# First chunk of a fused attention and MoE kernel: the gate's order, a copy of h, and where the weights' operations stand in a step

## The chip, the core and the metric

The kernel runs on one core of a Trainium2 chip. The metric is the device time in microseconds (us), the median of a few executions. TensorE (PE in the rows; PEld is its loading of weights), VectorE (DVE), ScalarE (ACT), GpSimd (POOL) and SyncE (SP, which here only issues DMAs) each work through a queue of their own in order, and wait for one another by semaphores. ScalarE's queue also issues some of the DMAs (ACTq in the rows).

## What is computed

Block-sparse attention over 4 batches of 768 positions and 8 heads of 64, and then an MLP over the 3072 tokens:

```python
def _moe_ref(x, w_in, w_out) -> np.ndarray:
    h = x @ w_in
    g = h * (1.0 / (1.0 + np.exp(-1.702 * h)))
    return (g @ w_out).astype(np.float32)
```

with x the attention's output (3072 x 512), w_in 512 x 2048 and w_out 2048 x 512. The gate h * sigmoid(1.702 h) is computed as h * (1 + tanh(0.851 h)), and the factor 0.5 is put on the output. The weights arrive as 64-bit numbers whose two 32-bit words have to be made into one fp32 number, and each fp32 number is split into a high part that TensorE's fast format holds and the rest, so that a product takes three matmuls.

## The kernel before

The 3072 tokens are six chunks of 512. A chunk's MLP is 16 steps of one 128-wide slice f of the hidden dimension; over all chunks they are steps m = 0 to 95, and `tick(m)` writes one step. Step m computes h for its slice in PSUM bank 7 (`up`, 12 matmuls in two halves, L491 to L493; rows of the built order call that bank bank_92), applies the gate (`gate`: tanh by ScalarE at L499, then (tanh + 1) * h by VectorE at L500, which reads h from the bank), rounds g to its high part by ScalarE (`gate_hi`, L505), and multiplies the slice of the step before into the output's four banks (`down(m - 1, 0)`, 8 matmuls at L535 and L536 with the high part of g; `down(m - 1, 1)`, 4 matmuls at L531 with the rest of g, which VectorE makes at L513 at the start of a step, `gate_lo`). There is one bank for h in all chunks but the last, so `up(m + 1)` can't begin before all readers of step m's h are done.

While a chunk's MLP runs, the attention for the next chunk is laid between its steps by `plan`, in quarters of a step: scores (L260) and values (L331) on TensorE in one step, transposes of the probabilities (L306) and the turn of the result (L384) in the next. Through steps 1 to 11 the scores and values open the odd steps, the transposes and the turn the even ones. With them go VectorE's minima (L283) and ScalarE's exponentials (L290) in odd steps, and ScalarE's copies `pt` of the transposes (L310), two tiny factors, and the pair xhi (ScalarE, L391) and xlo (VectorE, L392) of the finished rows in even ones. From step 12 on the plan is denser and its parts stand in other quarters.

The first chunk has more to do: the weights are made ready in it. `weights` is a generator; each `next` of it issues one operation, and four make a tile: a shift on VectorE (L446, with a 512 KB DMA for a later tile from ScalarE's queue, L414); VectorE's rest of the tile before (L427, with a DMA that saves it in DRAM when it is a wout tile, L433); VectorE's merge (L452, with ScalarE's Abs of the next tile, L422, into one of three buffers `a`); VectorE's second merge (L456, with ScalarE's rounding cast that waits for it, L459). There are 32 tiles, 16 win that stay and 16 wout in a ring of three, and about seven of them are done before step 0. When the ring is full the generator yields without an operation. A step in the first chunk issues up to five of these operations at its end, and in steps without scores four more ahead of the gate (`n0`, `n1`). What is left is issued ahead of step 16. From step 16 on a step reads a saved wout tile back (`stream`, `split`, tiles `wst`, two buffers).

The functions that the diff touches:

Of the kernel before, what the change touches and what calls it, by code (L numbers as in the profile page):

```python
# [9 lines left out]
F32 = mybir.dt.float32  # L10
# [3 lines left out]
ALU = mybir.AluOpType  # L14
# [4 lines left out]
P = 128  # L19
# [5 lines left out]
DM = H * D  # L25
DF = 2048
NCT = DM // P
NF = DF // P
# [9 lines left out]
QT = 4  # L38
# [5 lines left out]
class Kernel:  # L44
# [448 lines left out]
            nc.tensor.matmul(h, wil[:, k], hi[:, k], start=False, stop=(k == NCT - 1))  # L493
        self.h = h

    def gate(self, m):
        nc = self.nc
        g = self.work.tile([P, CT], F32, name="g")
        nc.scalar.activation(out=g, in_=self.h, func=AF.Tanh, scale=0.851)  # L499
        nc.vector.scalar_tensor_tensor(out=g, in0=g, scalar=1.0, in1=self.h, op0=ALU.add, op1=ALU.mult)  # L500
        self.g[m] = [g]

    def gate_hi(self, m):
# [107 lines left out]

    def tick(self, m):

        n0, n1 = 0, 0
        if m < NF:
            heavy = any(part == self.scores for q in range(QT) for part, g in self.at.get(QT * m + q, ()))
            n0, n1 = (0, 5) if heavy else (4, 5)

        def run(n):
            for _ in range(n):  # L620
                next(self.conv, None)

        def finish(todo):
            for f in todo:
                f()

        moe = m < NC * NF
        self.gate_lo(m - 1)
        finish(self.begin(QT * m))
        if moe:  # L630
            self.up(m, range(0, 2))
        finish(self.begin(QT * m + 1))
        if moe:
            self.up(m, range(2, 4))
        run(n0)
        after = self.begin(QT * m + 2)
        if moe:
            self.gate(m)
        finish(after[:2])
        self.down(m - LAG, 0)  # L640
        if moe:
            self.gate_hi(m)
        finish(after[2:])
        finish(self.begin(QT * m + 3))
        self.down(m - LAG, 1)
        self.split(m + 1)
        self.stream(m + 3)
        run(n1)

    def first(self):  # L650

# [93 lines left out]
```

## Time and profile before

| what | value |
|---|---|
| median of 3 executions | 797.04 us (796.22 to 797.87) |
| the profiled execution's own time | 797.87 us |
| its span, first to last instruction | 796.2 us |
| PE busy | 742.6 us, 93% |
| DVE busy | 413.5 us, 52% |
| ACT busy | 377.4 us, 47% |
| mean granted clock of TensorE | 0.981 of full speed |

Busy shares are averages over the whole span. The first chunk's MLP runs from about 75 us (step 0) to 210 us (step 16 begins); there the three engines are loaded otherwise than later, since the weights' operations are all before that. A step's beginning is read off TensorE's first L491 of it: 87.32 for step 2, 101.77 for step 4, 118.43 for 6, 135.60 for 8, 151.67 for 10, 169.71 for 12, 188.72 for 14, 209.96 for 16.

### The profile page before, as it was taken

To read this page: it belongs to the slowest core of one execution; us is meant where nothing else is said; L and a number is where in the kernel's file an instruction comes from. 1 tells how busy PE (TensorE), PEld (TensorE's weight loads), DVE (VectorE), ACT (ScalarE), POOL (GpSimd) and SP (SyncE) were. 2 spreads that over 40 slices of the span, in tenths; PEclk is the share of its full clock that TensorE was granted. 3 is DMA by queue.
4 is the path that set the end of the run, shared out by engine and by line. 5 is a ranking of instruction groups with operands and counts; after the bars stand their busy time and mean duration, and the time that the engine had idled before them with its cause. 6 is when DMAs were issued, how large, how long until landed. Compare 5 with 4: busy or idle time off the path is not lost.

```text
span 796.2 us, 19245 instructions
## 1 busy us (share of the span) xinstructions
PE 742.6 (93%) x7584; PEld 574.4 (72%) x7584; DVE 413.5 (52%) x1076; ACT 377.4 (47%) x937; POOL 56.6 (7%) x85
## 2 busy tenths in 40 slices
PE   2567998998899999999999999999999999999996
PEld 0445876776677777778778787787787777788885
DVE  3387777887554444454444544544464443443332
ACT  0576565565445454454454445444554545333232
POOL 5122100001000000000000000000000000000000
PEclk9798999999999999999999999999999999999999
DMA  8999676767474355674354465453574231131212
GB/s 262 287 351 329 208 251 204 247 201 236 140 228 154 103 174 135 184 197 144 116 181 123 127 184 142 138 155 108 170 249 166 67 90 58 40 96 50 54 40 53
DMA packets 61116, 128.21 MB, mean 161 GB/s; under 512 B 7569, under 2 KB 26514, under 8 KB 60514
## 3 DMA queue, kind: packets, MB, share of 16 engines
q1 hardware_dynamic: 46882, 80.50, 34.3%
q0 software_dynamic: 7232, 25.51, 9.8%
q10 hardware_dynamic: 6912, 20.97, 8.0%
q8 instruction: 60, 0.98, 0.5%
q14 instruction: 30, 0.25, 0.1%
HBM read 116.47 MB, written 10.49 MB: 159 GB/s over the span
## 4 chain that ended last, share of the span: by engine, by line
PE 76%; DVE 9%; ACT 6%; DMA 4%; issue 3%; ACTq 1%; POOL 0%; SPq 0%; POOLq 0%; DVEq 0%
PE bank L491 10%; PE bank L531 10%; PE bank L535 10%; PE bank L536 9%; PE bank L493 9%; PE bank L492 9%; PE bank L306 5%; PE bank L260 4%; PE bank L331 4%; ACT ex L290 2%; DMA ws<-a 2%; PE bank L339 2%; PE bank L272 2%; DVE a L452 2%; DVE a L456 2%
## 5 line engine op out<-in xcount | busy, mean ns | idle before, releaser
L500 DVE SCALAR_TENSOR_TENSOR g<-g,bank 128x512 f32<-128x512 f32 x96 | 66.0, 687 | 199.0 <-ACT g L499 198.9
L491 PE MATMUL bank<-xhi,win 128*128 128x512 f32 x384 | 159.5, 415 | 5.9 <-DVE g L500 5.7
L535 PE MATMUL bank<-wout,ghi 128*128 128x512 f32 x384 | 154.8, 403 | 0.0
L536 PE MATMUL bank<-wout,ghi 128*128 128x512 f32 x384 | 152.6, 397 | 2.2 <-DVE wout L427 2.2
L290 ACT ACTIVATE ex<-bank,nm 128x256 f32<-128x256 f32 (+1 forms) x208 | 99.5, 491 | 113.8 <-DVE nm L283 112.0
L493 PE MATMUL bank<-xhi,win 128*128 128x512 f32 x384 | 151.7, 395 | 0.2 <-DVE win L427 0.2
L492 PE MATMUL bank<-xlo,win 128*128 128x512 f32 x384 | 150.8, 393 | 0.0
L499 ACT ACTIVATE g<-bank 128x512 f32<-128x512 f32 x96 | 57.4, 598 | 145.1 <-PE bank L493 142.0
L531 PE MATMUL bank<-wout,glo 128*128 128x512 f32 x384 | 108.2, 395 | 0.5 <-DVE glo L513 0.5
L480 DVE TENSOR_TENSOR wout<-wst,wout 128x512 fp32r<-128x512 f32 x80 | 55.4, 692 | 84.1 <-ACT wout L479 83.1
L491 PEld LDWEIGHTS bank<-xhi,win 128*128 128x128 f32 x384 | 72.6, 189 | 24.1 <-DVE g L500 7.8
L283 DVE CUSTOM_DVE_ANT_1 bank<-bank,bias 128x256 f32<-128x256 f32 x176 | 73.8, 440 | 25.5 <-PE bank L260 17.3
L505 ACT CAST ghi<-g 128x512 fp32r<-128x512 f32 x96 | 59.7, 621 | 56.2 <-DVE g L500 56.2
L536 PEld LDWEIGHTS bank<-wout,ghi 128*128 128x128 f32 x384 | 72.9, 190 | 18.3 <-DVE wout L427 2.6
L531 PEld LDWEIGHTS bank<-wout,glo 128*128 128x128 f32 x384 | 72.7, 190 | 18.3 <-DVE glo L513 1.0
L493 PEld LDWEIGHTS bank<-xhi,win 128*128 128x128 f32 x384 | 72.6, 189 | 17.2 <-DVE win L427 0.6
L535 PEld LDWEIGHTS bank<-wout,ghi 128*128 128x128 f32 x384 | 72.5, 189 | 16.1
L492 PEld LDWEIGHTS bank<-xlo,win 128*128 128x128 f32 x384 | 72.9, 190 | 13.2
L216 POOL DMA_INDIRECT vown<-in_v_dram,vidx x44 | 43.3, 984 | 508.8 <-PE bank L331 397.4
L260 PE MATMUL bank<-kg,qt 64*32 64x256 f32 x1408 | 54.8, 409 | 20.4 <-DMA kg<-in_kb_dram 13.6
L310 ACT COPY pt<-bank 128x512 f32<-128x512 f32 (+1 forms) x120 | 61.2, 563 | 20.2 <-PE bank L306 19.7
L513 DVE TENSOR_TENSOR glo<-g,ghi 128x512 fp32r<-128x512 f32 x96 | 65.7, 685 | 1.4 <-ACT ghi L505 1.4
(73 smaller groups left out, 782.4 us busy)
## 6 DMA issues: line engine op xcount, KB each, us to landing
wst<-ws SPq DMA_DIRECT2D x80, 256.0 KB
kg<-in_kb_dram SPq DMA_DIRECT2D x136, 128.0 KB
kg<-in_kb_dram SPq DMA_DIRECT2D x22, 384.0 KB
raw<-in_moe_w_in_dram ACTq DMA_DIRECT2D x16, 512.0 KB
raw<-in_moe_w_out_dram ACTq DMA_DIRECT2D x16, 512.0 KB
kg<-in_kT_dram SPq DMA_DIRECT2D x4, 1536.0 KB
vown<-in_vd_dram SPq DMA_DIRECT2D x8, 768.0 KB
qt<-in_q_dram SPq DMA_DIRECT2D x22, 256.0 KB
```

The source lines that it names most:

```text
L260: nc.tensor.matmul(sps[h][BLK * c:BLK * (c + 1), n * i:n * (i + 1)].rearrange("p (n s) -> p n s", s=BLK), self.qt[r][rows, bi, UT * pair + ...
L283: nc.vector.tensor_tensor_reduce(out=at, in0=at, in1=bias, scale=-SCALE, scalar=3.0e38, op0=ALU.add, op1=ALU.min, accum_out=un["nm"][:, ha ...
L290: nc.scalar.activation(out=ex, in_=sps[h][:, n * k:n * (k + 1)], func=AF.Exp, bias=un["nm"][:, half, c:c + 1], scale=-1.0, accum_out=un["r ...
L310: copies.append(lambda pt=pt, ps=ps, m=m: nc.scalar.copy(out=pt[:, 0:m], in_=ps[:, 0:m]))
L491: nc.tensor.matmul(h, wih[:, k], hi[:, k], start=(k == 0), stop=False)
L492: nc.tensor.matmul(h, wih[:, k], lo[:, k], start=False, stop=False)
L493: nc.tensor.matmul(h, wil[:, k], hi[:, k], start=False, stop=(k == NCT - 1))
L500: nc.vector.scalar_tensor_tensor(out=g, in0=g, scalar=1.0, in1=self.h, op0=ALU.add, op1=ALU.mult)
L513: self.nc.vector.tensor_tensor(out=glo, in0=g, in1=ghi.bitcast(F32), op=ALU.subtract)
L531: nc.tensor.matmul(o[n], glo[:, tk[n]], woh, start=False, stop=last)
L535: nc.tensor.matmul(o[n], ghi[:, tk[n]], woh, start=(f == 0), stop=False)
L536: nc.tensor.matmul(o[n], ghi[:, tk[n]], wol, start=False, stop=False)
```

## The change

In the first chunk's steps 0 to 12 ScalarE copies h out of the bank right after tanh, into a buffer of the pool `wst`, and the gate's product reads that copy; in steps 13 to 15 and in all later chunks it reads the bank as before. The weights' operations of a step are put in three places: three right after the first quarter's pt copies and factors (only in steps without scores; the xhi and xlo pair now comes after them), three between tanh and the gate's product, and three at the step's end. That is 6 in a step with scores and 9 in one without; before, it was 5 and 9.

```diff
-    def gate(self, m):
+    def gate(self, m, between):
         nc = self.nc
         g = self.work.tile([P, CT], F32, name="g")
         nc.scalar.activation(out=g, in_=self.h, func=AF.Tanh, scale=0.851)
-        nc.vector.scalar_tensor_tensor(out=g, in0=g, scalar=1.0, in1=self.h, op0=ALU.add, op1=ALU.mult)
+        h = self.h
+        if m < NF - 3:
+
+            h = self.work.tile([P, DM], F32, name="wst")
+            nc.scalar.copy(out=h, in_=self.h)
+        between()
+        nc.vector.scalar_tensor_tensor(out=g, in0=g, scalar=1.0, in1=h, op0=ALU.add, op1=ALU.mult)
         self.g[m] = [g]
...
-        n0, n1 = 0, 0
+        n0, n1, n2 = 0, 0, 0
         if m < NF:
             heavy = any(part == self.scores for q in range(QT) for part, g in self.at.get(QT * m + q, ()))
-            n0, n1 = (0, 5) if heavy else (4, 5)
+            n0, n1, n2 = (0, 3, 3) if heavy else (3, 3, 3)
...
         moe = m < NC * NF
         self.gate_lo(m - 1)
-        finish(self.begin(QT * m))
+        after = self.begin(QT * m)
+        finish(after[:3])
+        run(n0)
+        finish(after[3:])
         if moe:
             self.up(m, range(0, 2))
         finish(self.begin(QT * m + 1))
         if moe:
             self.up(m, range(2, 4))
-        run(n0)
         after = self.begin(QT * m + 2)
         if moe:
-            self.gate(m)
+            self.gate(m, lambda: run(n1))
         finish(after[:2])
         self.down(m - LAG, 0)
         if moe:
...
         self.split(m + 1)
         self.stream(m + 3)
-        run(n1)
+        run(n2)
```

TensorE's and GpSimd's instructions keep their order; VectorE has as many as before in another order, ScalarE 13 more. Two places show the move. In the rows `bank_92` is h's bank, `win_101` to `win_116` are the win tiles 0 to 15, `wout_117` to `wout_119` the ring.

ScalarE in step 10 (an even one, without scores), before, from the pt copies to the high part of g:

```order
L310 COPY pt<-bank_85 128x512
L310 COPY pt<-bank_86 128x512
L391 CAST xhi_122<-bank_87 128x4x64
L414 DMA raw<-in_moe_w_in_dram 128x1024
L433 DMA ws_79<-a 128x512
L422 ACTIVATE a<-raw 128x512
L459 CAST win_113<-a 128x512
L499 ACTIVATE g<-bank_92 128x512
L505 CAST ghi<-g 128x512
```

and the same stretch now:

```order
L310 COPY pt<-bank_85 128x512
L310 COPY pt<-bank_86 128x512
L422 ACTIVATE a<-raw 128x512
L459 CAST win_113<-a 128x512
L414 DMA raw<-in_moe_w_out_dram 128x1024
L391 CAST xhi_122<-bank_87 128x4x64
L499 ACTIVATE g<-bank_92 128x512
L504 COPY wst<-bank_92 128x512
L422 ACTIVATE a<-raw 128x512
L459 CAST wout_119<-a 128x512
L511 CAST ghi<-g 128x512
```

The cast of win tile 12, which stood right ahead of tanh, now stands two places earlier; behind tanh comes the copy of h, and between it and the high part of g an Abs and a cast of the next tiles. On VectorE the same step went from shift, rest, merge, merge ahead of the gate's product to three operations ahead of xlo and three behind it.

VectorE in step 14, before, from its x to the minima of step 15; `wout_119` here is wout tile 14, which `down(14)` in step 15 reads:

```order
L373 TENSOR_TENSOR x<-bank_87,ri 128x256
L500 SCALAR_TENSOR_TENSOR g<-g,bank_92 128x512
L446 TENSOR_SCALAR a<-a 128x512
L427 TENSOR_TENSOR win_116<-a,win_116 128x512
L452 SCALAR_TENSOR_TENSOR a<-raw,a 128x512
L456 SCALAR_TENSOR_TENSOR a<-raw,a 128x512
L446 TENSOR_SCALAR a<-a 128x512
L513 TENSOR_TENSOR glo<-g,ghi 128x512
```

and now:

```order
L373 TENSOR_TENSOR x<-bank_87,ri 128x256
L446 TENSOR_SCALAR a<-a 128x512
L427 TENSOR_TENSOR wout_119<-a,wout_119 128x512
L452 SCALAR_TENSOR_TENSOR a<-raw,a 128x512
L506 SCALAR_TENSOR_TENSOR g<-g,bank_92 128x512
L456 SCALAR_TENSOR_TENSOR a<-raw,a 128x512
L427 TENSOR_TENSOR wout_117<-a,wout_117 128x512
L519 TENSOR_TENSOR glo<-g,ghi 128x512
```

The rest of wout tile 14 now stands in step 14, ahead of the gate's product; before, it stood behind the gate's product of step 15. The last tile's rest (`wout_117`) is issued in step 14 too, and no weights' operation is left behind it.

## Rows read from the trace of the kernel before

**Rows 1.** Busy time by stretch, steps 2 to 16, two steps a row

```profile
core 0: us, PE busy (x) PEld busy (x) DVE busy (x) ACT busy (x) POOL busy (x), PEclk, DMA share, GB/s
87.32:101.77 14.45, 14.45 (x157) 11.42 (x156) 10.70 (x27) 7.85 (x20) 2.67 (x2) 1.00 0.78 241
101.77:118.43 16.66, 15.21 (x157) 11.34 (x155) 13.35 (x31) 9.71 (x23) 0.00 (x0) 1.00 0.75 245
118.43:135.60 17.17, 14.93 (x154) 11.45 (x155) 13.04 (x31) 9.88 (x23) 1.88 (x2) 1.00 0.72 231
135.60:151.67 16.07, 15.26 (x154) 11.36 (x154) 13.41 (x31) 9.86 (x23) 0.00 (x0) 1.00 0.73 227
151.67:169.71 18.04, 16.13 (x155) 12.62 (x155) 13.91 (x32) 10.48 (x24) 1.87 (x2) 0.91 0.68 215
169.71:188.72 19.01, 17.35 (x253) 13.10 (x251) 14.05 (x34) 10.82 (x26) 0.00 (x0) 1.00 0.68 208
188.72:209.96 21.24, 17.48 (x162) 12.67 (x155) 15.54 (x39) 11.11 (x30) 2.48 (x2) 0.92 0.62 198
```

**Rows 2.** Waits from 101.77 to 209.96: total us, times, longest

```profile
DVE g L500 <- ACT g L499: 13.6, 10, 2.3
...
PEld bank L491 <- DVE g L500: 7.4, 8, 2.1
...
DVE xlo L392 <- ACT xhi L391: 3.5, 4, 1.0
...
DVE wout L427 <- ACT wout L459: 2.4, 6, 0.7
...
DVE win L427 <- ACT win L459: 2.1, 6, 0.4
```

**Rows 3.** Timelines by engine, step 10: start, us, what, [idle before, releaser]

```profile
154.31 0.40 PE L493 MATMUL bank<-xhi,win 128*128 128x512 f32 x1
...
159.58 0.62 ACT L459 CAST win<-a 128x512 fp32r<-128x512 f32 x1 [2.19 <-DVE a L456]
160.11 0.59 ACT L499 ACTIVATE g<-bank 128x512 f32<-128x512 f32 x1
...
160.73 0.69 DVE L500 SCALAR_TENSOR_TENSOR g<-g,bank 128x512 f32<-128x512 f32 x1 [1.18 <-ACT g L499]
...
161.47 0.71 PE L491 MATMUL bank<-xhi,win 128*128 128x512 f32 x1 [1.91 <-DVE g L500]
```

**Rows 4.** Timelines of VectorE and TensorE in step 15

```profile
205.00 0.68 DVE L427 TENSOR_TENSOR wout<-a,wout 128x512 fp32r<-128x512 f32 x1
...
205.74 0.62 PE L536 MATMUL bank<-wout,ghi 128*128 128x512 f32 x1 [2.15 <-DVE wout L427]
```

**Rows 5.** Forms of L500, L480 and L310: busy us, mean ns, idle before

```profile
L500 DVE SCALAR_TENSOR_TENSOR g<-g,bank 128x512 f32<-128x512 f32 x96 | 66.0, 687 | 199.0 <-ACT g L499 198.9
...
L480 DVE TENSOR_TENSOR wout<-wst,wout 128x512 fp32r<-128x512 f32 x80 | 55.4, 692 | 84.1 <-ACT wout L479 83.1
...
L310 ACT COPY pt<-bank 128x512 f32<-128x512 f32 x88 | 47.4, 591 | 20.2 <-PE bank L306 19.7 <-ACT wout L459 0.3 <-issue 0.2
```

**Rows 6.** Timelines of ScalarE and TensorE in steps 13 and 15

```profile
184.29 0.66 ACT L422 ACTIVATE a<-raw 128x512 f32<-128x512 f32 x1 [2.47 <-DMA ws<-a]
...
199.16 1.58 PE L260 MATMUL bank<-kg,qt 64*32 64x256 f32 x32 [1.28 <-ACT pt L310]
```

**Rows 7.** Saving DMAs and the Abs behind them: chain, then ScalarE's timeline

```profile
177.93 6.28 DMA ws<-a
...
101.72 0.33 ACTq L433 DMA_DIRECT2D ws<-a  x1
...
105.38 0.69 ACT L422 ACTIVATE a<-raw 128x512 f32<-128x512 f32 x1
...
128.59 0.97 ACTq L433 DMA_DIRECT2D ws<-a  x1
...
136.37 0.67 ACT L422 ACTIVATE a<-raw 128x512 f32<-128x512 f32 x1 [0.17 <-DMA ws<-a]
```

## The prediction

> **What bounds the kernel now.** The page gives TensorE 93% of the span, so I went to the stretches where it isn't gapless: the windows of two steps each through the first chunk. Steps 2 and 3 took 14.45 us with TensorE busy for all of it, and that is the floor for two such steps. The next four pairs hold the same TensorE work and took 16.66, 17.17, 16.07 and 18.04 us, 67.94 in place of 57.80; the two after them, 19.01 and 21.24 [rows 1]. VectorE is the busiest beside TensorE there: 13.04 to 13.91 us a pair.
>
> The waits say what fills the rest. Over 101.77 to 209.96 (six pairs) VectorE waits 13.6 us for tanh ahead of the gate's product, 3.5 for xhi, and 2.4 + 2.1 for the weights' casts: 2.27 + 1.33 us a pair [rows 2]. With its mean busy time in the four pairs, (13.35 + 13.04 + 13.41 + 13.91) / 4 = 13.43, that makes 17.03 a pair, and the four took 16.98 on average. So VectorE is never free there: it works, or stands at the gate's product, or waits for a rounding. TensorE follows it, and waits 7.4 us for h's bank [rows 2].
>
> Step 10 shows how. Its last h matmul starts at 154.31 and lasts 0.40, so h is there at 154.71. But tanh starts only at 160.11: ahead of it in ScalarE's queue stands a weights' cast that itself stood 2.19 us for VectorE's merge. The product at 160.73 lets go of the bank, and the next step's first matmul starts at 161.47 after 1.91 us of nothing [rows 3]. The granted clock then drops; its mean is 0.91 in that pair, which is 0.09 x 18.04 = 1.6 us of TensorE's time [rows 1].
>
> **The change, part by part.**
>
> *The gate's order and the copy.* In odd steps (with scores) VectorE now has three weights' operations between tanh and the product instead of none, in even ones three as well, with the other three ahead of xlo. Three operations are about 2 us of VectorE's work, as one pass over 128 x 512 takes 0.69 [rows 5]; tanh and copy are 0.59 + 0.59 [rows 3, 5]. So the 2.27 us a pair of waiting for tanh is covered. I take all of it away; the lower end is that it only moves to another instruction. The bank is let go by ScalarE's copy, not by the product, so TensorE's wait for it goes in steps 1 to 13, unless tanh is itself late. In odd steps tanh still stands behind four exponentials, and there 0.59 of copy replaces 0.69 of product, hardly a gain by itself; the exponentials only come sooner because VectorE does.
>
> *One more operation a pair.* 6 + 9 = 15 weights' operations a pair instead of 5 + 9 = 14: at most 0.69 us more of VectorE, the same total being done earlier.
>
> *Four pairs.* 16.98 - 2.27 + 0.69 = 15.4 us, against the floor of 14.45; times four is 61.6, so -6.3 us. The ends: 0 if the wait returns elsewhere, -10.1 at the floor. Steps 2 and 3 are on the floor already: 0.
>
> *Thirteen copies.* 128 x 512 from PSUM by ScalarE: 0.59 us [rows 5], 13 x 0.59 = 7.7 us. I cost them at nothing, since ScalarE is busy for 9.71 to 10.48 us of a pair [rows 1] and 1.2 more leaves 3.7 of 15.4. What lies behind a copy in the queue is a cast or an Abs, then the rounded g, which `down` reads only in the next step. If that cover were gone, the price is up to 7.7.
>
> Does the product get cheaper with h in SBUF? It took 687 ns with h in PSUM; a pass of the same shape with both inputs in SBUF took 692 [rows 5]. I take 0. [...]
>
> *Steps 12 to 16.* 19.01 + 21.24 us [rows 1]. In step 15 the rest of wout tile 14 runs at 205.00, behind that step's gate; TensorE waits 2.15 us for it [rows 4], and the clock's mean in that pair is 0.92, another 0.08 x 21.24 = 1.7 [rows 1]. The new order has this operation one step earlier, ahead of step 14's product: -3.8 us, the firmest single term. Two more stalls lie here: 2.47 us of ScalarE at an Abs in step 13, which waits for a saving DMA out of its buffer, with tanh and the pt copies behind it, and 1.28 us of TensorE for pt copies in step 15 [rows 6]. The second stood behind a weights' cast that is now done earlier. I credit 0.9 of these 3.7 us, as the Abs in step 13 now again stands ahead of the pt copies. Together -4.7; the ends are 0 and -7.5. In steps 13 to 15 there is no copy, so three operations delay the bank; they cover the tanh, and step 14's following `down` of 12 matmuls hides the rest: 0.
>
> *Later chunks* keep their order: 0. *DMAs*: the same ones, from the same queues, closer together; the DMA share was 0.78 in the pair that ran at the floor [rows 1], so the pace itself is affordable.
>
> *Sum.* -6.3 - 4.7 = -11.0. From the profiled execution, 797.87, that is 786.9; it lies 0.83 above the median 797.04, from which it is 786.0. I predict **786.0**; with both ends, 779.4 to 797.
>
> **Rivals.**
>
> *The saving DMAs eat half of it (792.5).* Abs of a new tile needs a buffer whose saving DMA has landed. One save took 6.28 us and one 7.8 (issued 128.59, its Abs at 136.37 waited for it until then), yet another Abs ran 3.66 us after its save without waiting [rows 7]. In the new order save and Abs are five operations apart, evenly laid: 5 / 15 x 15.4 = 5.1 us. If all took 6.28, each costs ScalarE 1.2 us, with some 1.9 saves a pair 2.2; with half of it passed on to VectorE a pair takes 16.5. Then the four pairs give -2 and the end some -2.5: 792.5.
>
> *All waits gone (779.4).* Every pair at 14.45 and all three stalls of the end away: -10.1 - 7.5. Against it: VectorE would have 14.12 us of work in 14.45.
>
> *The change doesn't free the bank sooner (797).* If tanh stays as late as before, behind the exponentials and the first three operations' cast, copy and product end alike and VectorE waits elsewhere. For it: in step 10 a cast still stands ahead of tanh in the new order. Against it: three operations instead of four lie ahead, and the product has others to cover it.
>
> *Slower, by the same saves (801).* If a save lands after 8.2 us, an Abs waits 3.1, 5.9 us a pair; half of it on VectorE makes 15.4 + 2.95 = 18.35, 5.5 more over the four pairs, and 1.5 or so comes back at the end. It decides from where half of 1.9 x (landing - 5.1) is more than the 1.6 us gained a pair: 6.8 us for the mean save. One of the three shown is above that.
>
> *Slower, by the copies (804.7).* [...] As a mechanism of this kernel: the copies lie on the path and bring nothing, 13 x 0.59 = 7.7 us. The rows speak against it, because what is waited for is the bank and tanh's place in the queue, not the pass.
>
> **How the numbers follow.** Chances: the forecast (780.5 to 791) 0.60; half eaten 0.20; floor 0.06; no change 0.06; slower by saves 0.05; slower by copies 0.03. The first two make the range, 780.5 to 794, which leaves 0.2 out. 0.2% of the time is 1.6 us, about what a measurement of this kernel can tell from no change. Faster by more than that 0.86, within 0.06, slower 0.08.
>
> **What the changed profile would show.** In the four middle pairs, 15 to 16 us each, found between TensorE's first L491 of steps 4, 6, 8, 10 and 12. In the waits of that stretch, the gate's product for tanh from 13.6 us to under 4, and L491's wait for h's bank under 2. No wait of `down(14)` for wout tile 14, and step 16 beginning near 199. VectorE's busy time the same, ScalarE's 7 to 8 us more. The prediction is wrong if the Abs' waits for saving DMAs grow past about 1 us a save, if the pairs stay above 16.5, or if a new wait of TensorE for the rest of g (L531) appears, since VectorE would then be late by its own work.

## The result, and the profile of the changed kernel

The changed kernel takes 785.01 us (median of 782.75 to 786.06), the kernel before 796.63 us in the same comparison (795.33 to 797.87). The ratio is 0.9851, with a 95% interval of 0.9822 to 0.9879. The forecast was 786.0.

The two profiled executions differ by 15.1 us of span (796.2 to 781.1), more than the medians do (11.6), since that of after is the quickest of its runs and that of before the slowest of its own. The 15.1 lie in four places, read off TensorE's first L491 of a step: 0.77 ahead of step 4, 7.82 in the four pairs of steps 4 to 11, 6.14 in steps 12 to 16, 0.37 behind that.

The windows of the changed kernel, two steps a row, with the columns of [rows 1] and the boundaries at its own steps:

```profile
86.56:101.00 14.44, 14.44 (x157) 11.43 (x156) 12.53 (x30) 10.07 (x24) 1.87 (x2) 1.00 0.87 258
101.00:115.45 14.45, 14.45 (x157) 11.43 (x156) 11.95 (x29) 10.03 (x25) 0.00 (x0) 1.00 0.80 249
115.45:131.08 15.63, 15.23 (x158) 11.35 (x156) 14.08 (x33) 10.69 (x26) 2.39 (x2) 1.00 0.79 260
131.08:145.55 14.47, 14.47 (x155) 11.45 (x155) 13.59 (x33) 10.97 (x25) 0.00 (x0) 1.00 0.77 254
145.55:161.12 15.57, 15.18 (x158) 11.34 (x156) 12.86 (x30) 10.58 (x25) 2.75 (x2) 1.00 0.77 244
161.12:180.65 19.53, 17.95 (x251) 13.25 (x251) 16.53 (x38) 13.65 (x30) 0.00 (x0) 1.00 0.78 256
180.65:195.23 14.58, 14.58 (x161) 11.52 (x155) 10.87 (x32) 8.79 (x26) 2.34 (x2) 1.00 0.67 210
```

Two of the four pairs stand on the floor of 14.45 us, and two are 1.1 to 1.2 above it. The last row is gapless, where before it held the wait for wout tile 14, and the granted clock is 1.00 in all rows. The pair of steps 12 and 13 is now the longest and 0.5 us longer than before.

The waits from 101.00 to 195.23, to be read beside [rows 2]:

```profile
DVE g L506 <- ACT g L499: 1.4, 1, 1.4
DVE g L506 <- ACT wst L504: 0.3, 1, 0.3
...
DVE xlo L392 <- ACT xhi L391: 4.4, 5, 1.2
...
PEld bank L491 <- ACT wst L504: 0.6, 2, 0.3
...
PE bank L260 <- ACT pt L310: 1.5, 2, 1.3
...
ACT a L422 <- DMA ws<-a: 2.6, 4, 1.0
```

The product's wait for tanh went from 13.6 to 1.4 us (0.3 more for the copy), TensorE's wait for h's bank from 7.4 to 0.6. The Abs waited 2.6 us for saving DMAs, in four waits. Of the prediction's other signs, step 16 begins at 195.2 (near 199 was forecast), and ScalarE's busy time over the whole span is 383.5 us against 377.4, so 6.1 more and not 7 to 8.

The timeline of step 10, to be read beside [rows 3]:

```profile
148.16 0.40 PE L493 MATMUL bank<-xhi,win 128*128 128x512 f32 x1
...
151.01 0.62 ACT L459 CAST win<-a 128x512 fp32r<-128x512 f32 x1 [1.42 <-DVE a L456]
...
151.80 0.60 ACT L499 ACTIVATE g<-bank 128x512 f32<-128x512 f32 x1
...
152.29 0.59 ACT L504 COPY wst<-bank 128x512 f32<-128x512 f32 x1
...
153.44 0.50 PE L491 MATMUL bank<-xhi,win 128*128 128x512 f32 x1
...
154.20 0.68 DVE L506 SCALAR_TENSOR_TENSOR g<-g,wst 128x512 f32<-128x512 f32 x1
```

Tanh still stands behind a cast that waited for VectorE, and starts 3.24 us after h is there (5.40 before). But the product doesn't wait, since VectorE had the three operations to do, and the next step's matmul starts ahead of the product, 0.56 us after the copy's end.

Wout tile 14's rest and its reader, in VectorE's and TensorE's timelines (steps 14 and 15), beside [rows 4]:

```profile
184.45 0.69 DVE L427 TENSOR_TENSOR wout<-a,wout 128x512 fp32r<-128x512 f32 x1
...
192.43 0.39 PE L541 MATMUL bank<-wout,ghi 128*128 128x512 f32 x1
```

It is there 7.3 us ahead of its reader, which waits for nothing. The stall that is left is in step 12, in TensorE's timeline:

```profile
165.43 1.58 PE L260 MATMUL bank<-kg,qt 64*32 64x256 f32 x32 [1.30 <-ACT pt L310]
```

The forms of the product and of the copy, beside [rows 5]:

```profile
L506 DVE SCALAR_TENSOR_TENSOR g<-g,bank 128x512 f32<-128x512 f32 x83 | 57.1, 687 | 183.8 <-ACT g L499 183.8
...
L506 DVE SCALAR_TENSOR_TENSOR g<-g,wst 128x512 f32<-128x512 f32 x13 | 8.9, 686 | 4.0 <-ACT wst L504 4.0
L504 ACT COPY wst<-bank 128x512 f32<-128x512 f32 x13 | 7.7, 594 | 0.0
```

### The profile page after: what moved, and what is told of

Its sections match the earlier page's. It is cut to its first block, busy times and chain, and to the rows that moved or that the text cites. A ratio compares the mean times of both kernels' runs of the same rounds, so it can differ in the third digit from the quotient of the medians.

```text
span 781.1 us, 19264 instructions
## 1 busy us (share of the span) xinstructions
PE 738.6 (95%) x7584; PEld 571.7 (73%) x7584; DVE 412.8 (53%) x1076; ACT 383.5 (49%) x950; POOL 57.1 (7%) x85
## 4 chain that ended last, share of the span: by engine, by line
PE 78%; DMA 7%; DVE 7%; ACT 4%; issue 2%; SPq 1%; ACTq 0%; DVEq 0%
PE bank L491 11%; PE bank L541 10%; PE bank L542 10%; PE bank L537 10%; PE bank L493 10%; PE bank L492 10%; PE bank L260 5%; PE bank L306 4%; PE bank L331 4%; DMA ws<-a 3%; DMA kg<-in_kb_dram 2%; PE bank L339 2%; PE bank L272 2%; DMA raw<-in_moe_w_in_dram 2%; DVE a L452 1%
## 5 line engine op out<-in xcount | busy, mean ns | idle before, releaser
L491 PE MATMUL bank<-xhi,win 128*128 128x512 f32 x384 | 158.4, 412 | 1.2 <-ACT xhi L391 0.9
L506 DVE SCALAR_TENSOR_TENSOR g<-g,bank 128x512 f32<-128x512 f32 x83 | 57.1, 687 | 183.8 <-ACT g L499 183.8
L480 DVE TENSOR_TENSOR wout<-wst,wout 128x512 fp32r<-128x512 f32 x80 | 55.4, 693 | 79.7 <-ACT wout L479 78.7
L491 PEld LDWEIGHTS bank<-xhi,win 128*128 128x128 f32 x384 | 72.1, 188 | 18.7 <-ACT xhi L391 1.1
L542 PEld LDWEIGHTS bank<-wout,ghi 128*128 128x128 f32 x384 | 72.5, 189 | 15.6
L310 ACT COPY pt<-bank 128x512 f32<-128x512 f32 (+1 forms) x120 | 61.1, 563 | 19.4 <-PE bank L306 19.3
L331 PEld LDWEIGHTS bank<-vown,pt 128*32 128x32 f32 x1408 | 43.8, 113 | 31.8 <-ACT pt L310 16.0
```

Source lines behind the costliest of these rows:

```text
L310: copies.append(lambda pt=pt, ps=ps, m=m: nc.scalar.copy(out=pt[:, 0:m], in_=ps[:, 0:m]))
L331: nc.tensor.matmul(av[BLK * c:BLK * (c + 1), 0, 2 * i + h], g["pt"][h][:, 2 * i + k, BLK * c:BLK * (c + 1)], src[:, at:at + D], start=(k = ...
L491: nc.tensor.matmul(h, wih[:, k], hi[:, k], start=(k == 0), stop=False)
L542: nc.tensor.matmul(o[n], ghi[:, tk[n]], wol, start=False, stop=False)
```

## The experiments

The theory behind the forecast was: VectorE sets the pace, the operations between tanh and the product fill its wait, the copy frees the bank, and the fifteenth operation a pair brings wout tile 14 in time. The rivals give the whole gain to one of these parts. The table has all kernels. "Steps 4 to 11" and "12 to 15" are windows of TensorE between its first weight load at L491 of steps 4, 12 and 16; "products" is the time from the gate's product of step 3 to that of step 11 on VectorE, four pairs of VectorE's own pace.

| kernel | median us (range) | ratio to before | steps 4 to 11 | 12 to 15 | products |
|---|---|---|---|---|---|
| before | 796.63 (795.33 to 797.87) | 1 | 67.93 | 40.05 | 67.10 |
| changed | 785.01 (782.75 to 786.06) | 0.9851 (0.9822 to 0.9879) | 60.15 | 33.88 | 62.47 |
| the same again | 785.26 (784.14 to 790.22) | 0.9862 (0.9827 to 0.9897) | 59.73 | 33.88 | 62.10 |
| copy alone | 801.79 (801.31 to 803.29) | 1.0084 (1.0066 to 1.0101) | 70.54 | 40.00 | 70.23 |
| order, no copy | 784.95 (783.82 to 785.94) | 0.9864 (0.9842 to 0.9885) | 63.97 | 31.37 | 64.37 |
| copy made, not read | 785.83 (785.21 to 786.83) | 0.9854 (0.9826 to 0.9883) | 63.83 | 32.03 | 64.40 |
| two copies | 791.62 (790.26 to 793.76) | 0.9939 (0.9915 to 0.9964) | 63.82 | 35.41 | 64.31 |
| 14 a pair | 783.88 (783.75 to 785.17) | 0.9860 (0.9838 to 0.9881) | 57.81 | 36.45 | 59.59 |
| 14, no copy | 785.38 (782.45 to 786.58) | 0.9845 (0.9813 to 0.9876) | 57.86 | 35.75 | 58.96 |
| 14, then 16 | 785.25 (783.17 to 787.96) | 0.9854 (0.9829 to 0.9879) | 57.81 | 39.07 | 59.56 |
| 14, then 15 | 783.95 (779.41 to 785.61) | 0.9830 (0.9800 to 0.9861) | 57.82 | 33.82 | 58.79 |
| n0 late | 786.66 (785.36 to 787.13) | 0.9886 (0.9867 to 0.9905) | 63.42 | 33.87 | 65.48 |
| steps without scores | 791.75 (788.58 to 792.60) | 0.9929 (0.9905 to 0.9953) | 62.67 | 37.99 | 63.72 |
| steps with scores | 787.76 (786.73 to 790.10) | 0.9892 (0.9869 to 0.9914) | 62.23 | 34.90 | 62.22 |

The windows are of one profiled execution each, so the medians and the windows need not agree to the tenth. Each ratio is to the kernel before in runs on the same chip. Its median there was 796.63 us for the changed kernel; 796.19 for the copy alone, the order alone, 14 a pair and n0 late; 796.96 for two copies, the two kernels with one kind of step, and "14, then 16"; 797.23 for the other four. Gains below are against these, so small differences between kernels of different rows are better read from the ratios.

**The copy alone.** The kernel before, with this:

```diff
-        nc.vector.scalar_tensor_tensor(out=g, in0=g, scalar=1.0, in1=self.h, op0=ALU.add, op1=ALU.mult)
+        h = self.h
+        if m < NF - 3:
+            h = self.work.tile([P, DM], F32, name="wst")
+            nc.scalar.copy(out=h, in_=self.h)
+        nc.vector.scalar_tensor_tensor(out=g, in0=g, scalar=1.0, in1=h, op0=ALU.add, op1=ALU.mult)
```

> The kernel before with the copy alone: steps 1 to 13 copy h to SBUF by ScalarE behind tanh and the product reads the copy; the weights' operations keep their places. Theory (VectorE paces a pair, and the copy only pays once VectorE's wait for tanh is filled): the pair stays near 17 us, the product still waits some 13 us for tanh in all, now also for the copy; 793 to 798 us. Rival (what TensorE waits for is the bank, and the copy alone gives it back): the 7.4 us of waits of the first h matmul go, 789 to 791 us. Rival (copies cost): 13 x 0.59 = 7.7 us more, 804 us.

It is slower than before, by 5.6 us, so the rival that gives the gain to the copy is refuted, and the theory's range (793 to 798) was too low as well: 801.79 lies nearer to the rival with the full price (804), as the copy costs 5.6 of the 7.7 us. Step 10 in its timelines of ScalarE, VectorE and TensorE shows why:

```profile
164.03 0.62 ACT L459 CAST win<-a 128x512 fp32r<-128x512 f32 x1 [2.13 <-DVE a L452]
164.55 0.59 ACT L499 ACTIVATE g<-bank 128x512 f32<-128x512 f32 x1
165.04 0.58 ACT L504 COPY wst<-bank 128x512 f32<-128x512 f32 x1
165.65 0.69 DVE L505 SCALAR_TENSOR_TENSOR g<-g,wst 128x512 f32<-128x512 f32 x1 [1.66 <-ACT wst L504]
...
165.67 0.80 PE L491 MATMUL bank<-xhi,win 128*128 128x512 f32 x1 [2.38 <-ACT wst L504]
```

VectorE's waits for the product from step 4 to step 11, eight products, in the kernel before and then with the copy alone:

```profile
DVE g L500 <- ACT g L499: 8.5, 7, 1.4
```

```profile
DVE g L505 <- ACT wst L504: 11.6, 8, 1.8
```

The copy's end releases the product and TensorE at the same instant (165.65 and 165.67). The bank is free 1.12 us after tanh's start; it was 1.36 in [rows 3], so 0.24 is gained on TensorE, while VectorE stands 0.48 longer at this product (1.66 against 1.18) and 3.1 longer at the eight. VectorE's four pairs went from 67.10 to 70.23, which is the same 3.1, and TensorE's followed. The granted clock has a share in TensorE's: its mean over steps 4 to 11 is 0.95, against 0.97 before.

**The order alone.** The changed kernel without the copy (`h = self.h` stays, the lines of the copy go).

> The changed kernel without the copy: three weights' operations between tanh and the product, which reads h from its bank. Theory: VectorE's wait for tanh (2.27 us a pair) is covered, but the bank is now let go by a product that stands behind three operations, so some of it comes back as TensorE's wait for the bank: 787 to 791 us, between the two kernels and nearer to the changed one. Rival (the order alone is all of the gain): 785 us, with no wait for the bank. Rival (the copy is what matters): 795 us or more, with the bank's wait at 7 us or more.

784.95: the rival is right on the time, all of the gain is the order's (still with 15 operations a pair). It isn't right on the bank. TensorE waits for it in steps 4 to 11, and VectorE no longer waits for tanh at all there. The waits of that stretch have this row, and the windows of steps 4 to 11 and 12 to 15 follow:

```profile
PEld bank L491 <- DVE g L502: 3.5, 3, 1.6
```

```profile
103.18:167.15 63.97, 60.07 (x618) 46.77 (x617) 53.72 (x125) 39.17 (x91) 5.15 (x4) 0.97 0.78 251
167.15:198.52 31.37, 31.37 (x407) 24.47 (x405) 25.49 (x66) 20.64 (x53) 2.35 (x2) 1.00 0.71 230
```

So without the copy the four pairs take 3.8 us longer than in the changed kernel (63.97 against 60.15), and steps 12 to 15, gapless here, 2.5 less. What the copy gives early it loses late. Not all of the 3.8 is waiting: behind a wait for the bank of 1.42 us the granted clock fell, and its mean of 0.97 over the four pairs is 0.03 x 63.97 = 1.9 us of TensorE's time, where the changed kernel has 1.00:

```profile
157.00:162.00 5.00, 3.58 (x43) 2.76 (x33) 4.93 (x12) 1.91 (x3) 2.75 (x2) 0.70 0.71 187
```

**Fourteen operations a pair.** The changed kernel with `(0, 3, 2)` in steps with scores.

> The changed kernel with two instead of three weights' operations at the end of a step with scores, so 14 a pair as before. Theory: the pairs of steps 4 to 11 are as long as in the changed kernel or up to 0.4 us shorter (VectorE has 0.69 us less), but the rest of wout tile 14 falls into step 15 again and TensorE waits some 2 us for it: 786 to 789 us. Rival (the fifteenth operation is most of the gain): 791 us or more. Rival (VectorE's work is still what paces a pair): 782 to 784 us.

783.88, the changed kernel's time within the uncertainty. The theory's range (786 to 789) was missed, the rival of the fifteenth operation (791) falls, and the rival by which VectorE's work still paces a pair has the time (782 to 784). The windows show two opposite effects, the first forecast by that rival, the second by the theory:

```profile
101.98:159.79 57.81, 57.81 (x619) 45.70 (x617) 50.62 (x118) 41.78 (x96) 4.42 (x4) 1.00 0.79 260
159.79:196.24 36.45, 33.39 (x407) 24.55 (x405) 28.59 (x72) 22.54 (x57) 2.39 (x2) 1.00 0.71 228
```

and the waits of the second of them have this one:

```profile
PE bank L541 <- ACT wout L459: 1.6, 1, 1.6
```

All four pairs are on the floor, 2.3 us less than with fifteen (0.58 a pair, where the theory allowed up to 0.4); then wout tile 14's cast is late in step 15 and steps 12 to 15 take 2.6 more.

**The place of n0.** The changed kernel with `run(n0)` back behind the h matmuls, directly ahead of the gate.

> The changed kernel with the three operations of an even step's beginning back behind the h matmuls, directly ahead of the gate, as the kernel before has its four. Theory: their place ahead of the last part of xlo matters little, since VectorE is not idle at either: 784 to 787 us. Rival (ahead of xlo they fill the wait for xhi): that wait, 4.4 us in five in the changed kernel, grows by some 2 us and the time to 788 us or more.

786.66, inside the theory's range at its upper end; ranges overlap with the changed kernel's. The four pairs are 3.3 us longer in the profile, not by the mechanism of the rival (the wait for xhi there is 2.5 us, as in the changed kernel) but by transposes that wait for exponentials, in steps 4 to 11:

```profile
PEld bank L306 <- ACT ex L290: 3.8, 7, 1.1
...
DVE a L446 <- ACT a L422: 3.6, 2, 2.1
```

The first is 1.9 in the changed kernel. VectorE's own four pairs take 3.0 us longer (65.48 against 62.47), and most of that is the second row, its shift's wait for ScalarE's Abs, which is 1.5 in the changed kernel. That a VectorE that is late makes the exponentials and with them the transposes late fits both rows; it was not tried by itself.

**One kind of step at a time.** The kernel before with four operations of a step without scores moved between tanh and the product (`(0, 0, 5)` with scores, `(0, 4, 5)` without), and with three of a step with scores moved there (`(0, 3, 2)` with, four ahead of the gate and five behind without).

> The kernel before, with one edit in the steps without scores alone: their four weights' operations stand between tanh and the product instead of ahead of tanh. No copy, 14 operations a pair, steps with scores as before. Theory (each of a pair's two waits for tanh is VectorE's own loss, and the gains of the two kinds of step add up to what the order alone gave, 11 us): these steps' waits of 0.7 to 1.2 us go, 791 to 794 us. Rival (only the steps with scores count, where the wait is 1.36 us and a step more often begins late): 796 us, no change. Rival (one kind of step is enough): 786 us.

> The kernel before, with one edit in the steps with scores alone: three of their five weights' operations of the end stand between tanh and the product, two stay. No copy, 14 operations a pair, steps without scores as before. Theory (the gains of both kinds add up): their waits of 1.36 us go, three of them beyond the four pairs, 788 to 791 us. Rival (these steps are nearly all): 785 to 786 us. Rival (the other kind): 796 us.

They gain 5.2 and 9.2 us, against 11.2 for the order alone, so each kind counts and the two overlap by some 3 us. The first theory's range held, the second's (788 to 791) was missed by 0.24 at its lower end, and that the gains add up did not hold. The product's waits for tanh from 101 to 210 us of each, first the one without scores, where the steps with scores still wait, then the other:

```profile
DVE g L502 <- ACT g L499: 10.4, 8, 1.4
```

```profile
DVE g L502 <- ACT g L499: 4.2, 5, 1.2
```

**Two copies.** The changed kernel with the copy written twice.

> The changed kernel with each copy of h made twice, into the same tile: 13 x 0.59 = 7.7 us more of ScalarE. It prices a copy where three operations of VectorE (2.0 us) stand between tanh and the product. Theory (tanh and one copy, 1.2 us, are covered by the three operations, and two copies, 1.8 us, barely; but the rounded g, Abs and casts behind them come later): 786 to 789 us. Rival (copies lie wholly on the path): 792 to 793 us. Rival (ScalarE has room to spare): 785 us.

791.62, 6.4 above the changed kernel's 785.26; the theory's range (786 to 789) is missed, and the full price (792 to 793) is 0.4 away. In steps 4 to 11 the bank is late again and casts too:

```profile
PEld bank L491 <- ACT wst L505: 4.0, 5, 0.9
...
DVE wout L427 <- ACT wout L459: 3.1, 3, 2.0
```

**The copy made and not read.** From the result of two copies I expected that one copy had a price too, paid back by the bank.

```diff
-            h = self.work.tile([P, DM], F32, name="wst")
-            nc.scalar.copy(out=h, in_=self.h)
+            nc.scalar.copy(out=self.work.tile([P, DM], F32, name="wst"), in_=self.h)
```

> The changed kernel with its thirteen copies of h made, but the product reads h from its bank, so that a copy costs ScalarE its 0.59 us and lets go of nothing. Theory (the copy has a price of some 0.5 us in ScalarE's order, as the second copy had, and the bank that it lets go of early pays that back, so that the two cancel): 790 to 792 us, with TensorE's waits for the bank at 3.5 us or more. Rival (neither counts: the copy is covered, and the early bank brings nothing): 785 us.

785.83: that theory falls. Thirteen copies that serve nothing are 0.9 us above the order alone (784.95) by the medians and nothing by the ratios (0.9854 and 0.9864), so no price can be told; in the windows -0.1 in steps 4 to 11 and 0.7 in 12 to 15. These windows are not a clean comparison, since the order alone's first one holds the drop of the clock and this one, at 1.00, none, while the wait for the bank, expected at 3.5 us or more, is longer here (it was 3.5 there):

```profile
PEld bank L491 <- DVE g L505: 4.6, 4, 1.6
```

The rival holds for the price; its other half, that the early bank brings nothing, is true of the whole but not of the four pairs (63.83 against 60.15).

**Order and 14 operations, no copy.** Against the kernel before only places differ.

> The order alone with 14 operations a pair: no copy, no fifteenth operation; against the kernel before only places are changed. Theory (the order is the gain, copy and fifteenth operation cancel each within themselves): 783.5 to 786.5 us, and its pairs of steps 4 to 11 a little above 14.45 us because of waits for the bank. Rival (without the copy the bank's waits need the fifteenth operation's earliness, or the other way round): 788 us or more.

785.38 and pairs on the floor; no wait for the bank shows in steps 4 to 11, less than expected. With 14 operations the product is early enough that the bank doesn't need the copy, though only just: product 3 ends 1.18 us before TensorE begins step 4, product 11 ends 0.07 us before step 12.

**A better distribution.** 14 a pair up to step 10, and from step 11 on four, or three, operations at the end of a step with scores (`2 if m < 11 else 4`, then `2 if m < 11 else 3`).

> The changed kernel with 14 operations a pair up to step 10, as in the run with fourteen, and two more at the end of each step with scores from step 11 on, so that wout tile 14 is ready before step 15. Theory (the fifteenth operation costs the four pairs some 2.3 us of TensorE's idleness, and brings as much back in steps 14 and 15; placed late, it brings without costing): steps 4 to 11 take 57.8 us, there is no wait for a wout tile, and the time is 782 to 783.5 us. Rival (steps 12 to 14 are then paced by the added operations): 784 to 786 us, as both before it.

> The changed kernel with 14 operations a pair up to step 10 and 15 from step 11 on, as the changed kernel has there. Theory (the run with two more from step 11 was too fast for the raw weights' loads there, behind which the pt copies stood; one more is not): steps 4 to 11 at 57.8 us, no wait for a wout tile in step 15, no wait of 2.6 us for the pt copies: 782 to 783.5 us, up to 2.3 below the changed kernel in the same call. Rival (what is saved early is lost between steps 12 and 16 whatever is done): the same as the changed kernel within 1 us.

With four the rival's range is met, 785.25, though by another wait than the added operations themselves: an Abs stands in ScalarE's queue until a load of the raw weights has landed, with the pt copies behind it, and TensorE waits for these in step 13 (timelines of ScalarE and TensorE):

```profile
176.33 0.66 ACT L422 ACTIVATE a<-raw 128x512 f32<-128x512 f32 x1 [1.77 <-DMA raw<-in_moe_w_out_dram]
176.89 1.06 ACT L310 COPY pt<-bank 128x512 f32<-128x512 f32 x2
...
177.52 2.64 PE L260 MATMUL bank<-kg,qt 64*32 64x256 f32 x32 [2.59 <-ACT pt L310]
```

With three, 783.95 lies 0.45 above the theory's range and 1.3 below the changed kernel, so neither range is met by the median. The profile, that of the fastest of its six executions (779.41), shows both gains together, no wait for a wout tile and little for the pt copies:

```profile
100.14:157.96 57.82, 57.82 (x619) 45.71 (x618) 51.08 (x119) 42.37 (x96) 3.99 (x4) 1.00 0.81 255
157.96:191.78 33.82, 32.66 (x407) 24.57 (x406) 29.19 (x73) 22.14 (x56) 2.35 (x2) 1.00 0.80 257
```

Steps 4 to 15 take 91.64 us, the changed kernel's 94.03 and 93.61 in its two profiles. The medians, 783.95 against 785.26 in the same comparison, go the same way by 1.3 us, but their ranges overlap; that it is the faster one is likely, not settled.

## Why the prediction was right, step by step

**VectorE is never free, and waits at the product: shown.** With only the places of operations changed (14, no copy) the four pairs went from 67.93 to 57.86 us; with only three operations of the steps with scores moved between tanh and the product, to 62.23. The chance that the wait only moves elsewhere came about in part: between the products of steps 3 and 11 the wait for tanh went from 8.5 us to none (0.3 for the copy), and VectorE's other waits for ScalarE rose from 4.9 to 7.1.

**The four pairs, -6.3 forecast, -7.8 measured: mis-sized.** VectorE's pace was forecast as 15.4 us a pair and is 62.47 / 4 = 15.6, so the sum held. Its parts did not, and that they make up for each other is luck: VectorE is busy for 54.34 us of the 62.47, 13.6 a pair where the sum has 14.1, and stands for 2.0 where it has 1.3. The step that failed is "TensorE follows it". With h copied, TensorE ran ahead: it starts step 4 0.5 us after product 3 has ended (99.75 + 0.69) and step 12 1.1 us before product 11 starts (161.12, 162.22). Such a lead is borrowed: in step 12 TensorE waits 1.30 us for pt copies, which stand in ScalarE's queue behind the rounding of that late product's g, an Abs and a cast, and steps 12 and 13 take 19.53 us, against 16.96 in the order alone. This fits the order alone being 3.8 longer in the four pairs and 2.5 shorter after them.

**One more operation a pair, forecast at most 0.69 us: too small in effect, and right in what it brings.** With 14 the four products take 59.59, with 15 62.47: 0.72 a pair on VectorE, as forecast. But it is the operation that takes the pairs off the floor (57.81 to 60.15), and the text treated the floor as out of reach (14.12 of VectorE's work in 14.45, chance 0.06). Even with 14 operations VectorE's four pairs do not fit in it, at 59.59 / 4 = 14.9: TensorE stays on the floor there by using up 1.8 us (59.59 - 57.81) of its distance to the product, which four pairs allowed; more pairs were not there to try.

**Thirteen copies, costed at nothing: right, though the reason given is not enough.** Made and not read they cost at most 0.9 us, which is not told from nothing. ScalarE's spare time was there in the other two kernels too: it works some 45 of the 70.54 us of steps 4 to 11 in the copy alone (39.91 before, and eight copies of 0.59) and some 47 of 63.82 with two copies (42.26 in the changed kernel, and eight more), both estimates. Yet there the copy alone cost 5.6, and a second one 6.4. The rows fit that it depends on whether the product or TensorE waits for the copy: 11.6 us of VectorE's waits in the copy alone, 4.0 of TensorE's with two copies. The forecast named the bank's release as one of two gains; the order alone gives the same median without it.

**Slower by the copies, 804.7, chance 0.03.** As a mechanism it is real, though not in the changed order: copy alone, 801.79 against 796.19 before, with 11.6 us of waits of the product for the copy in steps 4 to 11. The runs show besides that with other work between, thirteen copies cost nothing that can be told (785.83 made and not read, 784.95 without them).

**No cheaper product: shown.** 686 ns with h in SBUF (13 products), 687 with h in the bank (83 products), both in the changed kernel.

**Steps 12 to 16, -4.7 forecast, -6.1 measured: mis-sized by the credit for the other stalls.** The wait for wout tile 14 (2.15) and the drop of the clock beside it went, the -3.8 of the forecast; steps 14 and 15 together are 6.7 us shorter, steps 12 and 13 0.5 longer. Of the 3.7 us of other stalls 0.9 was credited; the Abs of step 13 waited 0.51 us in place of 2.47 and the pt copies of step 15 none, while 1.3 in step 12 is new. With 14 operations a pair the wait is there again (1.6), so the tile's date hangs on the fifteenth operation and not, as the text has it, on the new places alone; what it gains there the pairs pay: 2.6 against 2.3.

**Saving DMAs eat half, chance 0.20: not so.** The longest wait of an Abs for one was 1.0 us and all in six pairs 2.6, about 0.4 a pair in place of the rival's 2.2. That a wait for DMA can become the limit shows at 16 operations, there for a load (1.77 us of an Abs, with 2.59 of TensorE behind it). A fourth buffer was not tried.

Not settled: why the copy's lead is lost so exactly that the medians agree, beyond the one stall in step 12, and where the 3.5 us lie by which the two profiled executions differ more than the medians. The text took 0.2% as what a measurement can tell from no change; the interval of the result is 0.28% to either side.

## What to carry to other kernels

Ahead of an instruction that waits for another engine it paid here to put other work of its own engine: the order of two queues gave the whole gain (11.2 us, the order alone), and a copy that only decouples added nothing once the order was right (785.01 with it, 784.95 without). If several parts of a change act on the same wait, try each alone: here one of them alone is slower than before (801.79 against 796.19), one alone is the whole gain, and the third (the fifteenth operation) moves some two microseconds from one stage to another (2.3 and 2.6). Count the work of the second engine against the first one's floor, pair by pair, and put what does not fit where the first engine has more of its own.

## What the runs showed of the chip

In the two profiles of the changed kernel the first weight load of step 2 came at 86.54 and 88.85 us, and over all kernels between 85.71 us (14, then 15) and 90.08 us (two copies, with more copies ahead of it), as much as several of the effects above; stretches from step 4 on repeat better (60.15 and 59.73 for the same kernel), and were compared for that reason.

After a gap of 2.59 us at step 13 (14, then 16) the granted clock fell to 0.50 and stayed there until some 184 us while TensorE was busy without a gap; windows of that kernel:

```profile
175.00:178.00 3.00, 0.48 (x2) 0.18 (x2) 1.25 (x4) 1.67 (x4) 0.00 (x0) 0.85 0.91 289
178.00:180.00 2.00, 2.00 (x32) 1.24 (x30) 1.22 (x3) 0.91 (x3) 0.00 (x0) 0.50 0.40 152
180.00:182.00 2.00, 2.00 (x71) 1.74 (x65) 1.65 (x4) 0.45 (x1) 0.00 (x0) 0.50 0.00 0
182.00:184.00 2.00, 2.00 (x9) 1.62 (x6) 1.93 (x10) 1.20 (x5) 1.60 (x2) 0.52 0.36 68
184.00:186.00 2.00, 2.00 (x11) 1.59 (x10) 1.18 (x2) 0.81 (x5) 0.27 (x1) 1.00 0.93 257
```

Six us at 0.50 are 3 us of TensorE's time, and its busy time in steps 12 to 15 is 35.43 us there and 32.30 in the changed kernel, 3.1 more, which fits. After the changed kernel's gap of 1.30 us the clock stayed at 1.00 (its mean from 164 to 168 us). The length of the gap alone does not tell which it will be: behind 1.42 us in the order alone (157.50 to 158.92) it fell (0.70 on average from 157 to 162 us), behind 1.57 us in 14 a pair (191.51 to 193.08) it did not (1.00 over steps 12 to 15).
